# One core, attention and maxout feed-forward interleaved: the written order of commands, and the engines of copies, casts and masks, set anew

## The chip, the core and the metric

The kernel runs on one core of a Trainium2 chip. Five engines work side by side, each on its own queue in the order of the program: TensorE (PE, with its weight loads PEld), VectorE (DVE), ScalarE (ACT), GpSimd (POOL) and SyncE (SP). DMAs are issued from the queues of SP, ACT and POOL. The metric is the device time of one execution in microseconds; the median of six runs before the change is 200.44 us (199.77 to 200.55).

## What is computed

Attention with two kinds of heads, then a feed-forward layer whose hidden values are the largest of three products.

```python
scores = q @ k.T / sqrt(64)                      # 4 batches, 8 heads, 768 positions, 64 wide
keep = causal                                    # heads 0, 2, 6 ("retrieval")
keep = causal & ((key < 4) | (query - key < 64)) # the other heads
a = exp(where(keep, scores, -1e9) - max); a /= sum(a)
x = (a @ v), heads side by side                  # 3072 x 512
h = max(x @ w1, x @ w2, x @ w3)                  # 3072 x 768
out = h @ w_out                                  # 3072 x 512
```

Which heads are of which kind is read from the input `is_retrieval`, on the chip.

## The kernel before

**Tiles and steps.** A step `t` (0 to 15) is one batch `b`, one half of the positions (384 of 768, `half`) and one group of four heads; `t = 4 b + 2 half + group`. Within a step, `i` (0 or 1) is a pair of heads. The scores of a step are cut into units `u`: two units in the first half, four in the second. The feed-forward part `ffn(b, half)` works on 384 tokens: 18 products of a weight (768 columns in six blocks, three weights) with x, each four matmuls of 384 columns into one PSUM bank (line 437, 0.65 us), then three output blocks of six matmuls of 512 columns (line 473, 1.3 us). A product of the first weight is copied to `acc` by ScalarE or VectorE (line 454); the other two are joined to it by a maximum on VectorE (line 457), the last of which is `hT`. For batch 0 all products with w0 come first, then those with w1, then w2; for the others the three weights take turns.

**The order is written out by hand.** Nothing is scheduled: `PROGRAM` is a list of commands, and each command puts its instructions at the end of the queues of the engines that it uses, at the moment at which it stands in the list. Every queue so follows the order of the list. The commands:

- `read`, `flags`, `far`, `em hp`, `m hp`: from `is_retrieval` the flags of the heads, and on VectorE (line 388) two masks of 128x512 for heads 2hp and 2hp+1. `em` builds masks that TensorE adds to the scores (batch 0, first half), `m` masks that are multiplied in later. `far` also has two small POOL copies.
- `cast h hp e`: k and q of pair hp of batch 0 from fp32 to fp16 (line 211), by the engines in `e`, k first: `a` ScalarE, `d` VectorE, `p` POOL. `turnp h hp e`: six transposes on TensorE (line 230) and the copies to `KQ` (line 238), one of 768 columns for one letter, two of 384 for two. `h` is the half. `ld 1 hp`: loads of k and q of two pairs of the second half, issued by POOL.
- `load b g`, `turn b g i part`: for batches 1 to 3, k and q loaded as fp16 (two POOL DMAs, line 250), and a block transpose on VectorE (line 266); four per group.
- `load_v b half` (three SP DMAs), `load_vp` (three POOL DMAs), `v t i e`: v cast to fp16 (line 503, first letter) and multiplied by the flags into `vf` (line 505, second letter).
- `w n`: POOL's load of weight n (768 KB; 3 is w_out).
- `s t u [i] [b]`: score matmuls (line 552) into PSUM tile `st` (two buffers; with `b` into the four shared banks) and the exponential by ScalarE (line 563) into `pt`. For t = 0 and 1 the masks are added first by matmuls (line 536).
- `k t i u e`: mask multiplied into `pt`, on VectorE or POOL (line 585).
- `av t i [D]`: product with v (line 601), reciprocal (line 609) and scaling (line 611) on VectorE to `x`; with `D` a DMA transpose of x issued by SP (line 620), without it `x t i e` turns it on TensorE (line 633) and copies it (line 637). `x` of the last pair puts `ffn(b, half)` into the feed-forward queue.
- `f 1 e`: the next piece of the feed-forward queue (a product, an output block, or the empty half of an output block), its copy by engine `e`.
- `idle n`: n matmuls of zeros (line 321), work that nobody uses. `gate`: an SP DMA that waits for an exponential.

The four PSUM banks are shared by the feed-forward products, the transposes, the `av` results and the `b` scores. The loads of the first pairs stand ahead of `PROGRAM`, in `FIRST`: pair 0, the flags, pair 1, pairs 2 and 3, then v of the first half, on the queues of SP and ACT.

Of the kernel before, what the change touches and what calls it, by code (L numbers as in the profile page):

```python
# [713 lines left out]
```

## Time and profile before

| | |
|---|---|
| median of 6 runs | 200.44 us (199.77 to 200.55) |
| the profiled execution | 199.77 us, of which the span of the trace is 198.0 us |
| TensorE busy | 187.4 us (95%) |
| VectorE, ScalarE, POOL busy | 147.6, 114.6, 98.5 us (75%, 58%, 50%) |
| chain that ended last | PE 81%, DMA 6%, DVE 5%, POOL 2%, ACT 2%, issue 2%, SPq 1% |
| moved by DMA | 26.48 MB, 134 GB/s on average, 262 GB/s from 10 to 20 us |

Busy time is the union of the instructions' spans on an engine. The timeline and the chain give start and length in us; `x12` is the number of instructions merged into one row; square brackets hold the idle time ahead of an instruction and what ended it. In the chain, a piece stands with what it released next. All times are from the start of the span.

### The profile page before, as it was taken

The page shows a single profiled execution, that of the slowest core. Times are in us where ns is not written, and L with a number is a line of the kernel's source. Part 1 is how long each engine was busy: PE and PEld are TensorE (multiplying, and loading weights), DVE is VectorE, ACT ScalarE, POOL GpSimd, SP SyncE. Part 2 cuts the span into 40 slices and gives each one's busy share as a digit, 9 for nine tenths or more (in the row PEclk, how much of TensorE's full clock was granted, in tenths as well). Part 3 has the DMA queues.
Part 4 walks back from the last instruction along what each step waited for, and adds up shares of the span by engine and source line. Part 5 has one row for each costly group of instructions (what it writes and reads, how often), then busy time and mean ns, then how long its engine had stood idle before and what let it go on. Part 6 is the DMA issues. An engine that isn't in the chain of part 4 may idle for free.

```text
span 198.0 us, 5122 instructions
## 1 busy us (share of the span) xinstructions
PE 187.4 (95%) x2059; PEld 108.6 (55%) x2059; DVE 147.6 (75%) x306; ACT 114.6 (58%) x169; POOL 98.5 (50%) x132
## 2 busy tenths in 40 slices
PE   0998899999999999999999999999999999999992
PEld 0556555655555457664555457564565475745552
DVE  3787978798599968873897989897687537665740
ACT  3599885577857788277743976236457474102021
POOL 4685995968995704737942486910163127000000
PEclk9999999999999999999999999999999999999999
DMA  5999999989999264939991330214821330013004
GB/s 184 269 252 273 209 240 210 212 118 250 222 167 194 69 203 95 180 83 186 248 187 37 94 109 0 43 23 124 205 35 40 108 94 20 19 51 131 3 0 159
DMA packets 43245, 26.48 MB, mean 134 GB/s; under 512 B 33558, under 2 KB 38230, under 8 KB 43222
## 3 DMA queue, kind: packets, MB, share of 16 engines
q1 hardware_dynamic: 37206, 15.01, 31.7%
q0 software_dynamic: 4784, 10.23, 26.4%
q10 hardware_dynamic: 1232, 0.92, 1.5%
q8 instruction: 16, 0.26, 0.6%
q14 instruction: 7, 0.06, 0.1%
HBM read 25.17 MB, written 6.29 MB: 159 GB/s over the span
## 4 chain that ended last, share of the span: by engine, by line
PE 81%; DMA 6%; DVE 5%; POOL 2%; ACT 2%; issue 2%; SPq 1%; POOLq 0%
PE yy L437 43%; PE yy L473 14%; PE st L552 10%; PE oacc L601 10%; PE yst L437 3%; DMA qs<-in_q_dram 3%; DMA ks<-in_k_dram 2%; DVE mk L388 1%; DVE x L611 1%; DMA out_dram<-ot 1%; ACT pt L563 1%; PE yst L473 1%; DVE hT L457 1%; ACT ot L479 1%; POOL pt L585 1%
## 5 line engine op out<-in xcount | busy, mean ns | idle before, releaser
L563 ACT ACTIVATE pt<-st 128x1024 f16<-128x1024 f32 (+3 forms) x99 | 82.8, 895 | 37.1 <-PE st L552 28.7
L585 POOL TENSOR_TENSOR pt<-pt,mk 128x512 f16<-128x512 f16 (+1 forms) x51 | 53.8, 1077 | 34.8 <-ACT pt L563 34.2
L437 PE MATMUL yy<-xT,w1t 128*128 128x384 f16 x180 | 36.0, 326 | 0.0
L437 PE MATMUL yy<-xT,w0t 128*128 128x384 f16 x180 | 35.8, 326 | 0.0
L437 PE MATMUL yy<-xT,w2t 128*128 128x384 f16 x180 | 35.8, 326 | 0.0
L457 DVE TENSOR_TENSOR acc<-yy,acc 128x384 f16<-128x384 f32 x45 | 24.9, 554 | 11.2 <-PE yy L437 4.9
L473 PE MATMUL yy<-woutt,hT 128*128 128x512 f16 (+1 forms) x138 | 31.7, 375 | 0.0
L552 PE MATMUL st<-KQ 32*128 32x384 f16 (+5 forms) x560 | 28.6, 279 | 0.4
L457 DVE TENSOR_TENSOR hT<-yy,acc 128x384 f16<-128x384 f32 x45 | 24.6, 556 | 4.2 <-PE yy L437 1.7
L601 PEld LDWEIGHTS <-pt 128*128 128x128 f16 x672 | 24.2, 97 | 5.2 <-issue 1.5
L266 DVE STREAM_TRANSPOSE KQ<-kq 128x384 f32<-128x384 f32 x24 | 25.5, 1134 | 0.0
L454 ACT CAST acc<-yy 128x384 f16<-128x384 f32 x29 | 13.9, 486 | 20.0 <-PE yy L437 16.8
L601 PE MATMUL oacc<-va,pt 128*128 128x65 f16 x352 | 25.0, 193 | 0.4 <-POOL pt L585 0.4
L437 PEld LDWEIGHTS <-w0t 128*128 128x128 f16 x192 | 17.9, 98 | 13.1 <-issue 1.7
L437 PEld LDWEIGHTS <-w2t 128*128 128x128 f16 x192 | 17.8, 98 | 12.0 <-DVE x L611 0.3
L437 PEld LDWEIGHTS <-w1t 128*128 128x128 f16 x192 | 17.1, 97 | 11.4 <-issue 1.2
L552 PEld LDWEIGHTS <-KQ 32*128 32x128 f16 (+1 forms) x560 | 12.1, 93 | 18.5 <-issue 12.6
L473 PEld LDWEIGHTS <-hT 128*128 128x128 f16 x150 | 13.9, 98 | 14.9 <-issue 0.4
L601 PE MATMUL oacc<-vf,pt 128*128 128x65 f16 x320 | 21.5, 193 | 0.2 <-DVE vf L505 0.2
L505 POOL TENSOR_TENSOR vf<-va,far 128x384 f16<-128x384 f16 x13 | 10.9, 843 | 17.6 <-DVE va L503 8.6
L611 DVE TENSOR_TENSOR x<-oacc,rc 128x384 f16<-128x384 f32 x32 | 17.8, 557 | 1.1
L585 DVE TENSOR_TENSOR pt<-pt,mk 128x512 f16<-128x512 f16 (+1 forms) x35 | 18.2, 542 | 0.0
(75 smaller groups left out, 139.6 us busy)
## 6 DMA issues: line engine op xcount, KB each, us to landing
out_dram<-ot SPq DMA_DIRECT2D x23, 256.0 KB, 2.2
vs<-in_v_dram SPq DMA_DIRECT2D x21, 256.0 KB, 4.4
kq<-in_k_dram POOLq DMA_DIRECT2D x6, 384.0 KB, 6.1
kq<-in_q_dram POOLq DMA_DIRECT2D x6, 384.0 KB, 7.6
qs<-in_q_dram ACTq DMA_DIRECT2D x4, 192.0 KB, 3.9
ks<-in_k_dram SPq DMA_DIRECT2D x4, 192.0 KB, 3.7
ks<-in_k_dram POOLq DMA_DIRECT2D x2, 384.0 KB, 6.9
qs<-in_q_dram POOLq DMA_DIRECT2D x2, 384.0 KB, 7.3
```

The costliest lines, as they stand in the source:

```text
L266: nc.vector.transpose(out=dst.rearrange("c (p j) -> c j p", j=n)[:, j0:j1], in_=src.rearrange("c (j i) -> c j i", i=R),)
L388: nc.vector.tensor_scalar(out=mk[:, h], in0=kept, scalar1=least[:, h : h + 1], scalar2=-30000.0 if early else None, op0=ALU.is_le if early ...
L437: nc.tensor.matmul(yy[:, 0:HALF], w_t[wi][:, ks, ni * P : (ni + 1) * P], xT[b, half][ks].rearrange("p a t -> p (a t)"), start=(ks == 0), s ...
L454: copy_out[0](out=acc[ni], in_=yy[:, 0:HALF])
L457: nc.vector.tensor_tensor(out=dst, in0=yy[:, 0:HALF], in1=acc[ni], op=ALU.max)
L473: nc.tensor.matmul(yo[:, 0:n], hT[ns][:, tb * P : (tb + 1) * P], woutt[:, ns, c : c + n], start=(ns == 0), stop=(ns == NNB - 1),)
L505: vf_engine.tensor_tensor(out=vf[j][:, hs, k0:k1, 0:D], in0=vs[:, hs, 0:1] if half == 0 else va[j][:, hs, k0:k1, 0:D], in1=far[:, hs, k0:k ...
L552: nc.tensor.matmul(sts[g // m][:, g % m, c0 : c0 + n * P], KQ[rows, 0, ki * P : (ki + 1) * P], KQ[rows, 1, t0 : t0 + n * P], start=(c0 == ...
L563: nc.scalar.activation(out=pts[t, i][:, u, h0 : h0 + m, 0:w], in_=st[:, :, 0:w], func=AF.Exp, scale=sc,)
L585: engine.tensor_tensor(out=x, in0=x, in1=m, op=ALU.mult)
L601: nc.tensor.matmul(o[:, qi, hl, 0 : D + 1], pt[:, u, hl, c : c + P], vv[:, 2 * hp + hl, ki, 0 : D + 1], start=(idx == 0), stop=(idx == len ...
L611: nc.vector.tensor_tensor(out=x, in0=o[:, :, :, 0:D], in1=rc.unsqueeze(3).to_broadcast([P, HB, 2, D]), op=ALU.mult,)
```

## The change

`PROGRAM` is written anew. It holds the same commands for the same steps, 471 of them, with the same loads and the same tiles; what differs is their order and the engine letters of `cast`, `turnp`, `v`, `k`, `x` and `f`. No function changes. The new text is a line shorter, so lines of the code after it stand one lower (line 437 becomes 436).

Counted by letters, before to after: casts of k and q ScalarE 4 to 6, VectorE 5 to 4, POOL 7 to 6; casts of v ScalarE 5 to 12, VectorE 9 to 3, POOL 18 to 17; `vf` VectorE 10 to 8, POOL 22 to 24; `k` commands VectorE 31 to 26, POOL 43 to 48; `f` commands ScalarE 99 to 106, VectorE 93 to 86; `x` ScalarE 8 to 5, VectorE 4 to 7; copies to `KQ` of 384 columns ScalarE 10 to 2 and VectorE 2 to 6, of 768 columns ScalarE none to 3 and VectorE 2 to 1.

In order: the idle matmuls come ahead of the flags; `s 0 0 0` comes ahead of the first `s 1`; `ld 1 2` comes ahead of the first weight, `load_vp 0 1` ahead of `w 2`, `load 1 0` ahead of `w 3`; `turnp 1 2` and `turnp 1 3` come ahead of the first `f`; the `turn` commands of group (1, 0) come ahead of the first output block; `av 14 1` moves behind `av 15 0`.

```diff
 PROGRAM = (
-    "read, flags, cast 0 0 pa, cast 0 1 ad, cast 0 2 pp, em 0, turnp 0 0 aa, em 3, idle 8, far",
-    "ld 1 0, cast 0 3 ap, turnp 0 2 aa, em 2, turnp 0 1 dd, s 1 0 0, s 0 0 0, s 0 1 0 b, em 1",
-    "w 0, turnp 0 3 d, s 0 0 1, ld 1 2, s 1 1 0 b, s 0 1 1 b, v 0 1 dd, s 1 0 1, v 1 1 dd",
-    "s 1 1 1, v 0 0 dp, cast 1 1 pp, w 1, turnp 1 1 aa, cast 1 0 da, av 0 1, av 0 0, idle 2",
-    "av 1 1, turnp 1 0 aa, m 0, v 1 0 pp, s 2 0 1, w 2, av 1 0, s 2 0 0, x 1 1 d, x 1 0 d",
-    "x 0 1 d, x 0 0 a, s 2 1, m 1, m 2, m 3, cast 1 3 pd, f 1 d, load_vp 0 1, w 3, f 1 a, f 1 a",
-    "turnp 1 3 aa, cast 1 2 dd, load 1 0, f 1 d, s 2 2, k 2 1 1 p, f 1 a, k 2 0 1 p",
-    "turnp 1 2 d, f 1 d, k 2 0 2 d, f 1 a, s 3 0, k 3 0 0 d, f 1 d, f 1 d, s 2 3, k 2 1 2 p",
-    "f 1 d, f 1 a, f 1 d, k 2 0 3 d, load 1 1, f 1 a, v 2 1 pp, f 1 d, f 1 d, v 2 0 ad",
-    "v 3 1 ap, k 2 1 3 p, f 1 a, s 3 1 0, s 3 2 0, av 2 0 D, v 3 0 pp, s 3 1 1, f 1 d, av 2 1 D",
-    "k 3 0 1 p, f 1 a, turn 1 0 0 0, k 3 1 0 p, s 3 3 0, turn 1 0 0 1, turn 1 0 1 0, s 3 2 1",
-    "f 1 a, load_v 1 0, f 1 d, k 3 0 2 p, k 3 0 3 p, turn 1 0 1 1, f 1 a, k 3 1 1 p, s 3 3 1",
-    "k 3 1 2 p, gate, av 3 0, s 4 0, k 3 1 3 p, turn 1 1 0 0, f 1 a, av 3 1, turn 1 1 0 1",
-    "x 3 0 a, f 1 a, turn 1 1 1 1, k 4 0 0 p, x 3 1 a, f 1 d, k 4 1 0 p, s 4 1, f 1 a",
...
+    "cast 0 0 da, cast 0 3 pp, read, idle 8, flags, idle 2, em 3, ld 1 0, em 0, cast 0 1 aa",
+    "turnp 0 0 a, cast 0 2 aa, em 2, ld 1 2, s 0 0 0, far, turnp 0 1 a, em 1, w 0, v 0 0 pp",
+    "turnp 0 3 da, s 0 0 1, turnp 0 2 d, s 0 1 0 b, w 1, s 1 0 0, s 0 1 1 b, s 1 0 1, s 1 1 0 b",
+    "v 1 0 ad, cast 1 1 pp, cast 1 0 dd, v 0 1 ap, v 1 1 dp, turnp 1 0 dd, av 0 0, s 1 1 1",
+    "turnp 1 1 ad, av 1 0, cast 1 2 ap, load_vp 0 1, s 2 0 0, x 0 0 d, av 1 1, s 2 0 1, av 0 1",
+    "x 1 1 a, x 1 0 d, x 0 1 d, turnp 1 2 a, s 2 1, m 1, cast 1 3 pd, m 0, w 2, turnp 1 3 dd",
+    "k 2 0 1 p, m 3, f 1 d, s 3 0, f 1 a, k 2 1 1 p, f 1 a, s 2 2, load 1 0, f 1 d, m 2",
+    "k 3 0 0 d, f 1 a, k 2 1 2 d, f 1 d, f 1 d, s 2 3, k 2 0 2 p, w 3, f 1 a, s 3 1 0, f 1 d",
+    "f 1 a, k 2 1 3 p, v 2 0 ad, s 3 2 0, k 3 0 1 d, f 1 d, s 3 3 0, k 2 0 3 d, f 1 d, f 1 a",
+    "f 1 d, f 1 d, v 3 0 pp, v 2 1 pp, s 3 1 1, k 3 0 3 p, s 3 2 1, turn 1 0 0 1, load 1 1",
+    "f 1 d, turn 1 0 0 0, k 3 0 2 p, f 1 a, turn 1 0 1 0, turn 1 0 1 1, k 3 1 1 p, v 3 1 ap",
+    "f 1 a, av 2 0 D, av 3 0, s 3 3 1, av 2 1 D, s 4 0, gate, k 3 1 2 p, turn 1 1 0 0",
+    "k 3 1 3 p, k 3 1 0 p, load_v 1 0, load_v 2 0, f 1 a, av 3 1, s 4 1, turn 1 1 0 1, f 1 d",
+    "turn 1 1 1 0, x 3 0 a, f 1 a, turn 1 1 1 1, f 1 d, x 3 1 a, f 1 a, k 4 1 0 d, f 1 d",
...
+    "f 1 d, s 7 0, k 6 0 2 d, k 6 0 3 d, f 1 a, v 7 0 pp, load 2 1, f 1 a, f 1 a, v 7 1 ap",
+    "turn 2 0 1 0, s 7 1, k 6 1 1 p, turn 2 0 0 0, f 1 a, load_v 2 1, x 5 1 d, k 7 1 1 p, f 1 a",
+    "f 1 a, f 1 a, v 9 0 pd, v 8 0 dp, v 6 0 pp, k 6 1 2 p, turn 2 0 0 1, f 1 a, turn 2 0 1 1",
+    "s 7 2, f 1 a, f 1 a, load 3 1, f 1 d, k 7 1 2 p, f 1 d, turn 2 1 1 0, v 6 1 pp, s 7 3",
+    "f 1 a, load_v 3 0, av 6 0 D, f 1 d, k 7 1 3 p, f 1 a, f 1 a, f 1 d, k 7 0 2 p, f 1 a",
+    "f 1 a, s 8 0, turn 2 1 0 0, turn 2 1 0 1, f 1 a, k 7 0 1 p, k 7 0 3 p, f 1 d, turn 2 1 1 1",
+    "av 7 1 D, f 1 d, s 8 1, av 7 0 D, k 6 1 3 p, av 6 1 D, s 9 0, k 8 0 1 p, v 11 0 pd",
...
+    "f 1 d, k 15 1 3 p, f 1 a, f 1 a, f 1 d, f 1 d, k 15 0 1 p, k 15 0 2 p, f 1 d, av 15 1 D",
+    "f 1 d, av 15 0 D, av 14 1 D, x 15 1 a, f 1 a, f 1 a, f 1 d, f 1 a, f 1 a, f 1 d, f 1 a",
...
```

## The prediction

> **What bounds the kernel now.** I read the page first (busy shares and slices), then the busy time by stretches of 10 us, then the timeline and the chain of the first 50 us, then the landing times of the loads.
>
> ```profile
> span 198.0 us, 5122 instructions
> PE 187.4 (95%) x2059; PEld 108.6 (55%) x2059; DVE 147.6 (75%) x306; ACT 114.6 (58%) x169; POOL 98.5 (50%) x132
> ```
>
> The busy time by stretches (length, then PE, PEld, DVE, ACT, POOL, granted clock, DMA share, GB/s):
>
> ```profile
> 0.00:10.00 10.00, 5.26 (x36) 3.08 (x37) 5.54 (x23) 4.58 (x9) 5.35 (x17) 1.00 0.93 227
> 10.00:20.00 10.00, 9.23 (x128) 5.68 (x128) 7.75 (x22) 9.74 (x18) 6.71 (x12) 1.00 1.10 262
> 20.00:30.00 10.00, 9.12 (x79) 5.03 (x76) 8.77 (x20) 8.40 (x14) 9.58 (x12) 1.00 1.13 225
> 30.00:40.00 10.00, 9.84 (x117) 6.05 (x117) 7.73 (x16) 5.39 (x8) 7.38 (x9) 1.00 1.14 211
> 40.00:50.00 10.00, 9.53 (x122) 5.49 (x121) 9.43 (x14) 7.80 (x13) 7.75 (x9) 1.00 0.99 193
> 50.00:60.00 10.00, 10.00 (x124) 5.55 (x121) 7.37 (x16) 6.87 (x11) 9.92 (x16) 1.00 0.96 187
> ```
>
> From 50 us to 190 us TensorE is busy without a gap, and this work doesn't change. So only two things can move the end: how late the first 50 us leave TensorE, and a new gap after them. In the first 50 us ScalarE is full between 10 and 20 us (9.74 of 10) and the DMA engines are full throughout (share 0.93 to 1.14). The timeline (start, us, engine) and then the chain show the places that matter:
>
> ```profile
> 5.33 3.15 PE L321 MATMUL st<-zero 128*128 128x512 f16 x8
> 8.32 0.33 PE L230 MATMUL tr<-ident,kn 128*128 128x128 f16 x3
> 10.03 5.94 ACT L563 ACTIVATE pt<-st 128x1024 f16<-128x1024 f32 x11 [0.48 <-PE st L552]
> 20.71 2.11 PE L437 MATMUL yy<-xT,w0t 128*128 128x384 f16 x12
> 31.86 0.50 POOL L503 CAST va<-vs 128x384 f16<-128x384 f32 x1 [2.27 <-DMA vs<-in_v_dram]
> 45.36 0.20 PE L601 MATMUL oacc<-va,pt 128*128 128x65 f16 x1 [0.38 <-POOL pt L585]
> ```
> ```profile
> 34.94 0.83 DVE vf L505
> 44.15 1.17 POOL pt L585
> 48.34 2.17 PE yy L437 x12
> ```
>
> The reader is to see: the first exponential starts at 10.03; the products of the feed-forward part start at 20.71; the second v load is late (POOL waits 2.27 us for it at 31.86), so that `av 2 0` waits on VectorE's `vf`; and `av 3 1` waits on a POOL mask at 45. The row at 48.34 is the first product of `ffn(0,1)`; its first matmul stands at 48.28. In both programs the same TensorE work lies ahead of that product, so its start is my yardstick.
>
> The landing of a load is its issue (timeline) plus its time to landing (view of the tile):
>
> ```profile
> L402 POOL DMA_DIRECT2D w2t<-in_moe_w_dram x1: 803/803/803, 16.8 to 16.8; - x1
> DMA to landing us min/median/max: 11.6/11.6/11.6
> ```
>
> So w2 landed at 28.4; likewise w0 18.7, w1 24.6, the POOL v loads 29.6 to 31.7, woutt 35.2, the last early kq 42.8. These loads queue behind each other: 1.1 us per 256 KB, 3.3 to 4.1 per weight of 768 KB, 1.9 per kq.
>
> **The change part by part.** An engine that has work waiting starts its next instruction before the last one ends, so I take start-to-start times from back-to-back rows: ScalarE exponential of 1024 columns 0.92 (row 1.02), of 256 0.26, cast or copy of 384 columns 0.37 to 0.42; VectorE cast 0.46, max 0.47, block transpose 0.92 (row 1.13), reciprocal with multiply 0.70; POOL mask of 512 1.11, of 256 0.62, cast 0.46 to 0.53, `vf` 0.79, DMA issue 0.8 (0.55 for kq).
>
> *Start.* The eight idle matmuls (and the two that took 0.59 us at 16.2) move ahead of the first transposes, into time in which TensorE waited 4.6 us for its first work: they cost nothing there. Pair 0 is cast by VectorE and ScalarE at 4.0 to 4.9, turned at 5.6 (behind two more idle matmuls), copied by ScalarE at 6.4 to 7.15 behind two casts of pair 1, and `s 0 0 0` no longer waits for pair 2. Its exponential follows the casts of pair 2 at 7.9, 2.1 us earlier than 10.03. The row: eight idle matmuls took 3.15 us (about 0.42 apart), and 3.6 us after the first work at 4.7 the transposes ran at 0.056 apart. The Trainium skill (TensorE: Matmul & The Clock Gate, Part 1) says some 3.4 us of sustained work opens the full clock, with a window that runs freely. By the page's rule the first transposes of after may still be slow; six of them at 0.107 instead of 0.056 would be 0.3 us, which the wait for pair 1 on ScalarE covers.
>
> ScalarE pays for it. Ahead of the exponentials of `s 2 1` it casts six k or q tiles (four before: 0.84 more) and two v tiles (none before: 0.84); its copies are eight of 384 columns before (2.96), and three of 768 and two of 384 after. No row has a ScalarE copy of 768: the exponential of 768 (0.71) and two copies of 384 (0.74) bound it from above, one of 384 (0.37) from below; I take 0.7, the nearest in size, so 2.8 in all. I walked the queues in their new order with the times above. ScalarE: casts 5.95, copy 6.4, casts 7.06 and 7.48, exponential 7.9, copies 8.8 and 9.5, exponential 10.25, two short ones 11.2, then 12.1 (VectorE's copy of pair 2 ends at 11.55), 13.0, 13.55, 14.5 to 15.0, v casts to 15.8, then a wait to 17.0 because TensorE stands before `turnp 1 0` for qn, whose load is issued 0.7 us later than before (behind the casts of pair 3 on POOL, 9.0 instead of 8.3) and lands near 15.1; `s 2 0` at 18.3 and 19.2; `s 2 1` at 21.75. The first product starts at 22.3 (20.71 before, but with 0.68 us less TensorE work ahead of it): at this point after is 0.9 us behind.
>
> *Loads.* `ld 1 2` now stands ahead of w0, and the v loads ahead of w2 and woutt. POOL issues them at 10.6, w0 at 12.4, w1 at 14.0, v at 17.9, w2 at 21.0, kq at 25.0, woutt at 28.4. At the queue's rate: w0 21.0 to 21.4 (used 22.3), w1 24.7, v 25.8 to 28 (used 31), w2 31.6 to 32.3 (used 33.4), kq 35.3, woutt 38.8 (used 41.7). None is late, w0 and w2 by about 1 us only; the 2.27 us wait for v is gone.
>
> *22 to 48 us.* Walking TensorE with 0.66 per product, 0.54 per whole score group, 0.27 per single pair, 0.95 per `av`, 1.3 per output block: it waits 0.7 us before `s 3 0` (VectorE copies pair 3 only after two mask builds), reaches product (1,3) with its end at 31.5, `s 3 1 1` at 35.4, `av 2 0` at 38.0. VectorE has four block transposes between the last maxima, so the last hT is ready at 41.0; TensorE fills that time with three `av`. `s 4 0` ends at 41.7, the output blocks and `av 3 1` follow (POOL's last mask for it, after 11.2 us of POOL work from 30.4, ends at 41.6; needed at 43.0), and `ffn(0,1)` starts at 47.3. Before: 48.28. Gain 1.0 us. What it gains against product (1,3), where it's 0.35 behind, is the two waits shown above (`vf`, POOL mask) and the smaller ones around them.
>
> *After 48 us.* Masks, casts and copies change engines all over (POOL 48 masks for 43, VectorE 26 for 31; ScalarE 106 `f` for 99). TensorE's work is the same, and a later producer costs only if it comes after TensorE wants it. The tightest place: v 7 1 is a ScalarE cast placed after the second output block of `ffn(0,1)`, near 67.0 (47.3 and 19.7 of TensorE work). From its `vf` on (0.8) POOL has nine masks (10.0), two whole v preparations (2.5), two half ones (0.8) and a kq issue (1.15) in a row, 15.3 us, up to the end of mask `k 6 1 3`, which `av 6 1` wants right away, after 16.4 us of TensorE work, near 83.5. The mask ends at 82.7. Cost nothing, cover 0.8 us; if that cover is gone, what is over comes straight onto TensorE. The bound by rows: masks at 1.09 (the fastest) save 0.2, at 1.18 (the mean row) add 0.6. SBUF — State Buffer of the Trainium skill (section on ports) speaks against the change here: POOL shares a port pair with VectorE, held for a whole instruction. If the masks met this more often and ran at 1.25, 1.3 us would come on top and 0.5 would be lost; by the rows nothing is lost.
>
> At the end `av 14 1` is now the last one whose transpose goes by DMA; 4.55 us of TensorE work cover it against 0.75 on VectorE, a short queue on SP and 2.3 to 2.7 to landing. Cost nothing, cover about 0.9. The last 24 steps are the same.
>
> **Sum.** The profiled execution took 199.77 us (span 198.0 and 1.77 around it). Less 1.0 gives 198.8. The median of six runs, 200.44, is 0.67 above it, so I forecast 199.5 for the median: 1.0 earlier with 0.1 given back in the narrow places. 0.2% (0.4 us) is about what a measurement of this kernel can tell from no change.
>
> **The rivals.**
>
> *ScalarE and VectorE pay their full rows (slower).* Place: 8 to 45 us. If each instruction occupies its engine for its row (exponential 1.02, transpose 1.13, cast 0.51) the same walk has the last hT at 43.9 and `ffn(0,1)` at 49.7, 1.4 us later than before: 201.8. For it: 1.7 us more ScalarE work, and four block transposes more (two reciprocals with multiplies fewer) on VectorE ahead of the last hT. Against: eleven exponentials took 5.94 us at 10.03, less than their rows' 7.1. Between 1.0 earlier and 1.4 later it decides from about 40% of the difference between row and spacing.
>
> *POOL late near 83 us, or w2 late (no change).* A chain 10% longer or w2 a microsecond later takes 0.7 to 1.0 off: 200.2 to 200.5.
>
> *The start counts in full.* If `turnp 1 0` isn't held by its load, the 0.9 us behind at the first product fall away: about 198.4.
>
> *It doesn't matter.* If TensorE's filler hides start and v wait alike, 200.4. Against: TensorE has no spare after 50 us, so what it loses before stays lost.
>
> **How the numbers follow.** Forecast (198.8 to 200.0) 0.46; full start 0.10; no change by POOL, w2 or otherwise 0.17; slower by the row-length case or an unseen gap 0.27. The range takes in 198.4 and the slower rival short of its end: 198.3 to 201.7. Faster by over 0.2% 0.57, within it 0.16, slower 0.27.
>
> **What would show it.** First exponential near 7.9 instead of 10.0; first product near 22.3; no wait for v on POOL; `ffn(0,1)` near 47.3; TensorE busy 10.00 in every stretch from 50 to 180. Wrong if w0 or w2 is awaited by TensorE, if `yy` waits on VectorE around 37 to 42, or if `av 6 1` waits on POOL near 83.

## The result, and the profile after

The change made no difference that can be measured, where 199.5 us and a gain were forecast. The ratio of the times, after to before, is 1.0016 (95% interval 1.0000 to 1.0032). The median of before over 72 runs is 200.31 us. Of the 36 runs of after, the profiled one among them, 13 were disturbed (202.6 to 206.3 us, 11 of them at a mean granted clock of 0.98 to 0.992); the median of the 23 others is 200.29 us, and the times of the kernels below leave such runs out. The profiled execution of after took 200.29 us with a span of 198.6; before's took 199.77 and 198.0. So against the execution on which the forecast was summed, after is 0.5 us later instead of 1.0 us earlier.

The head of the page of after:

```profile
span 198.6 us, 5124 instructions
PE 189.1 (95%) x2059; PEld 108.4 (55%) x2059; DVE 147.4 (74%) x296; ACT 117.2 (59%) x173; POOL 102.1 (51%) x136
```

The busy time of after by stretches (columns as before), and behind it two stretches of before:

```profile
0.00:10.00 10.00, 7.08 (x41) 3.10 (x41) 5.21 (x23) 6.00 (x11) 3.31 (x12) 1.00 0.91 226
10.00:20.00 10.00, 8.39 (x116) 4.87 (x113) 7.04 (x15) 8.97 (x18) 8.84 (x17) 1.00 0.98 231
20.00:30.00 10.00, 9.06 (x79) 4.86 (x80) 8.44 (x19) 8.64 (x13) 7.95 (x10) 1.00 1.12 223
30.00:40.00 10.00, 10.00 (x101) 5.63 (x99) 9.93 (x19) 6.64 (x9) 8.59 (x11) 1.00 1.16 209
40.00:50.00 10.00, 10.00 (x153) 6.25 (x153) 9.85 (x20) 6.95 (x12) 4.51 (x5) 1.00 0.68 138
...
60.00:70.00 10.00, 10.00 (x128) 5.20 (x126) 9.85 (x20) 7.50 (x11) 3.34 (x6) 1.00 0.96 167
70.00:80.00 10.00, 9.58 (x100) 5.38 (x98) 5.20 (x10) 7.13 (x11) 9.83 (x14) 1.00 1.02 215
```
```profile
60.00:70.00 10.00, 10.00 (x104) 4.89 (x102) 9.93 (x20) 7.89 (x10) 5.94 (x7) 1.00 0.60 129
70.00:80.00 10.00, 10.00 (x140) 6.44 (x140) 7.61 (x17) 7.69 (x11) 2.91 (x4) 1.00 0.59 139
```

Two things are to be seen. From 30 to 50 us TensorE has no gap left (10.00 and 10.00, where before had 9.84 and 9.53): the waits there are gone, as forecast. And there is a new gap between 70 and 80 us, 9.58, where before was full. The DMA share at 60 to 70 us is 0.96; in before it was 0.60.

The yardstick, the first matmul of `ffn(0,1)`, and the products around it in the timeline of after:

```profile
22.95 0.81 PE L436 MATMUL yy<-xT,w0t 128*128 128x384 f16 x4
48.26 1.46 PE L436 MATMUL yy<-xT,w0t 128*128 128x384 f16 x8
78.55 0.81 PE L436 MATMUL yy<-xT,w0t 128*128 128x384 f16 x4
79.78 0.82 PE L436 MATMUL yy<-xT,w1t 128*128 128x384 f16 x4 [0.42 <-DVE x L610]
```

First product 22.95 (forecast 22.3, before 20.71 with 0.68 us less work ahead of it), `ffn(0,1)` 48.26 (forecast 47.3, before 48.28). The gap at 79.78 is ended by VectorE's `x` of `av 6 0`, which frees a PSUM bank. The chain of after, followed through that gap:

```profile
57.56 9.54 DMA vs<-in_v_dram
...
67.84 0.82 POOL vf L504
68.66 0.55 POOL kq L249
69.21 8.74 DMA kq<-in_q_dram
...
78.90 0.25 DVE rc L608
79.17 0.57 DVE x L610
...
79.78 2.12 PE yy L436 x12
```

and VectorE's block transpose in the timeline:

```profile
77.98 1.13 DVE L265 STREAM_TRANSPOSE KQ<-kq 128x384 f32<-128x384 f32 x1 [1.82 <-DMA kq<-in_q_dram]
```

So: a v load lands at 67.1; POOL, which had waited for it, prepares that v and only then issues the loads of kq (2,1); they land at 77.95; VectorE's block transpose waits 1.82 us for them, with `rc` and `x` of `av 6 0` queued behind it; TensorE waits for the bank.

To split the time I use the yardstick and the first matmul of the last output block of the kernel. The TensorE work between them is the same in every kernel here, and so is the work ahead of the first. The two ends in before, and then the second in after:

```profile
48.28 2.24 PE L437 MATMUL yy<-xT,w0t 128*128 128x384 f16 x12
193.00 0.82 PE L473 MATMUL yst<-woutt,hT 128*128 128x256 f16 x6
```
```profile
193.55 0.82 PE L472 MATMUL yst<-woutt,hT 128*128 128x256 f16 x6
```

Before needs 193.00 - 48.28 = 144.72 us from one to the other, after 193.55 - 48.26 = 145.29 us.

### The profile page after: what moved, and what is told of

Read it like the earlier page. It is cut to its first block, busy times and chain, and to the rows that moved or that the text cites. A ratio compares the mean times of both kernels' runs of the same rounds, so it can differ in the third digit from the quotient of the medians.

```text
span 198.6 us, 5124 instructions
## 1 busy us (share of the span) xinstructions
PE 189.1 (95%) x2059; PEld 108.4 (55%) x2059; DVE 147.4 (74%) x296; ACT 117.2 (59%) x173; POOL 102.1 (51%) x136
## 4 chain that ended last, share of the span: by engine, by line
PE 73%; DMA 14%; DVE 3%; ACT 2%; SPq 2%; issue 2%; POOL 2%; POOLq 0%; DVEq 0%; ACTq 0%
PE yy L436 38%; PE yy L472 13%; PE oacc L600 9%; PE st L551 8%; DMA vs<-in_v_dram 5%; DMA kq<-in_q_dram 4%; PE yst L436 3%; DMA ks<-in_k_dram 3%; DMA qs<-in_q_dram 2%; ACT pt L562 1%; DVE x L610 1%; PE yst L472 1%; SPq L285 1%; DVE KQ L237 1%; DVE va L502 1%
## 5 line engine op out<-in xcount | busy, mean ns | idle before, releaser
L584 POOL TENSOR_TENSOR pt<-pt,mk 128x512 f16<-128x512 f16 (+1 forms) x55 | 58.8, 1089 | 41.1 <-ACT pt L562 36.0
L456 DVE TENSOR_TENSOR acc<-yy,acc 128x384 f16<-128x384 f32 x45 | 24.4, 554 | 13.2 <-ACT acc L453 6.3
L472 PE MATMUL yy<-woutt,hT 128*128 128x512 f16 (+1 forms) x138 | 32.2, 375 | 0.0
L265 DVE STREAM_TRANSPOSE KQ<-kq 128x384 f32<-128x384 f32 x24 | 26.0, 1127 | 1.8 <-DMA kq<-in_q_dram 1.8
L600 PE MATMUL oacc<-vf,pt 128*128 128x65 f16 x320 | 20.9, 193 | 0.0
L584 DVE TENSOR_TENSOR pt<-pt,mk 128x512 f16<-128x512 f16 (+1 forms) x31 | 16.2, 547 | 0.9 <-ACT pt L562 0.6
L502 POOL CAST va<-vs 128x384 f16<-128x384 f32 x17 | 9.2, 544 | 11.5 <-DMA vs<-in_v_dram 11.5
```

The source lines that it names most:

```text
L265: nc.vector.transpose(out=dst.rearrange("c (p j) -> c j p", j=n)[:, j0:j1], in_=src.rearrange("c (j i) -> c j i", i=R),)
L456: nc.vector.tensor_tensor(out=dst, in0=yy[:, 0:HALF], in1=acc[ni], op=ALU.max)
L472: nc.tensor.matmul(yo[:, 0:n], hT[ns][:, tb * P : (tb + 1) * P], woutt[:, ns, c : c + n], start=(ns == 0), stop=(ns == NNB - 1),)
L502: op(out=vdst, in_=vs[:, hs])
L584: engine.tensor_tensor(out=x, in0=x, in1=m, op=ALU.mult)
L600: nc.tensor.matmul(o[:, qi, hl, 0 : D + 1], pt[:, u, hl, c : c + P], vv[:, 2 * hp + hl, ki, 0 : D + 1], start=(idx == 0), stop=(idx == len ...
```

## The experiments

**1. Which half of the list loses (c1, c2).** c1 has after's commands up to `x 3 1` and then before's; c2 has before's up to `x 3 1` and then after's. The seams (in kernels put together from two lists, line numbers stand one or two off those of after):

```diff
 c1, against after
-    "k 3 1 3 p, k 3 1 0 p, load_v 1 0, load_v 2 0, f 1 a, av 3 1, s 4 1, turn 1 1 0 1, f 1 d",
-    "turn 1 1 1 0, x 3 0 a, f 1 a, turn 1 1 1 1, f 1 d, x 3 1 a, f 1 a, k 4 1 0 d, f 1 d",
+    "gate, k 3 1 2 p, turn 1 1 0 0, k 3 1 3 p, k 3 1 0 p, load_v 1 0, f 1 a, av 3 1, s 4 1",
+    "turn 1 1 0 1, f 1 d, turn 1 1 1 0, x 3 0 a, f 1 a, turn 1 1 1 1, f 1 d, x 3 1 a, f 1 a",
+    "k 4 0 0 p, f 1 d, k 4 1 0 p, f 1 a, load_v 1 1, f 1 a, v 4 0 pp, k 4 0 1 d, k 4 1 1 p",
...
 c2, against before
-    "x 3 0 a, f 1 a, turn 1 1 1 1, k 4 0 0 p, x 3 1 a, f 1 d, k 4 1 0 p, s 4 1, f 1 a",
-    "turn 1 1 1 0, load_v 1 1, f 1 a, v 4 0 pp, k 4 0 1 d, k 4 1 1 p, f 1 a, s 5 0, v 4 1 pp",
+    "f 1 a, av 3 1, turn 1 1 0 1, x 3 0 a, f 1 a, turn 1 1 1 1, k 4 0 0 p, x 3 1 a",
+    "load_v 2 0, s 4 1, turn 1 1 1 0, k 4 1 0 d, f 1 d, f 1 a, k 4 1 1 d, f 1 a, s 5 0, f 1 a",
...
```

Expected of c1:

> The commands of after up to `x 3 1` (without `load_v 2 0`, which keeps its place of before), then those of before that are left. Theory A (the new start and middle gain nothing by 48 us, and all of the loss, 0.6 us, comes from one wait near 79 us that belongs to after's later order): `ffn(0,1)` begins near 48.3 as in before (48.28), no gap of TensorE near 79, span 197.9 to 198.2, ratio to before 0.999 to 1.001. Rival B (the loss is made by the start, where ScalarE and VectorE got more work, and only shows later): span 198.4 to 198.7, ratio 1.002 to 1.004. Rival C (the start gains the 1.0 us that was forecast, and the later order loses more): span near 197.0, ratio near 0.995.

Expected of c2:

> The commands of before up to `x 3 1`, then those of after that are left. Theory A: `ffn(0,1)` near 48.3, then the same gap of about 0.55 us near 79 as in after, where VectorE's block transpose waits for the kq load: span 198.4 to 198.7, ratio 1.002 to 1.004. Rival B: span near 198.0, no gap, ratio 0.999 to 1.001. Rival C: span near 199.5, ratio near 1.008.

Measured: c1 199.06 us, ratio 0.9948 (0.9923 to 0.9972), span 196.9, `ffn(0,1)` at 46.93. c2 201.23 us, ratio 1.0056 (1.0024 to 1.0088), span 199.7, `ffn(0,1)` at 49.02. My theory A, drawn from the one trace of after, fell with c1 (c2's interval alone leaves both A and C open); rival C stood: the head gains the forecast 1.0 us, and the later order loses about as much. Multiplied, the two ratios make 1.0004, within the interval of after's. In c2 the stretch from the yardstick to the last block takes 145.66 us, 0.94 more than before. It has two waits of TensorE, neither of them at the place of after's: one for a copy by ScalarE just behind the seam, and one for a DMA transpose of x.

```profile
50.95 0.64 PE L553 MATMUL st<-KQ 32*128 32x384 f16 x16 [0.34 <-ACT acc L455]
...
72.58 0.48 PE L438 MATMUL yy<-xT,w0t 128*128 128x384 f16 x2 [0.32 <-DMA xT<-x]
```

**2. Take away the late kq (c3, c7).** c3 issues kq (2,1) ahead of the POOL command that waits for v; c7 leaves POOL alone and exchanges two v loads on SP, so that the v POOL waits for comes first.

```diff
 c3, against after
-    "f 1 d, s 7 0, k 6 0 2 d, k 6 0 3 d, f 1 a, v 7 0 pp, load 2 1, f 1 a, f 1 a, v 7 1 ap",
+    "f 1 d, s 7 0, k 6 0 2 d, k 6 0 3 d, f 1 a, load 2 1, v 7 0 pp, f 1 a, f 1 a, v 7 1 ap",
...
 c7, against after
-    "k 3 1 3 p, k 3 1 0 p, load_v 1 0, load_v 2 0, f 1 a, av 3 1, s 4 1, turn 1 1 0 1, f 1 d",
+    "k 3 1 3 p, k 3 1 0 p, load_v 1 0, load_v 1 1, f 1 a, av 3 1, s 4 1, turn 1 1 0 1, f 1 d",
...
-    "k 5 1 0 d, f 1 a, s 5 1, f 1 d, f 1 a, v 4 0 pp, load_v 1 1, v 4 1 pp, av 4 0 D, s 6 0",
+    "k 5 1 0 d, f 1 a, s 5 1, f 1 d, f 1 a, v 4 0 pp, load_v 2 0, v 4 1 pp, av 4 0 D, s 6 0",
```

> After with `load 2 1` ahead of `v 7 0` instead of behind it; nothing else. Theory A (POOL's wait of 6.5 us for v holds the issue of the kq load, whose late landing at 78.0 stops VectorE's block transposes, with `rc` and `x` of `av 6 0` behind them): the two kq DMAs are issued near 61 instead of 68.6, land by 71, the block transposes don't wait, the gap of TensorE near 79 is gone; span 0.5 to 0.6 less than after's 198.6, so 198.0 to 198.1, ratio to before 0.999 to 1.001. Rival D (VectorE is late there by its own work, four block transposes and the mask builds, not by the load): gap stays at 0.3 or more, span 198.4 to 198.6.

> After with `load_v 1 1` and `load_v 2 0` exchanged, so that SP issues v of (1,1) first; the POOL commands keep their order, `load 2 1` behind `v 7 0`. Theory A, one step further back (v of (1,1) is late because v of (2,0), used 20 us later, stands ahead of it on SP): v of (1,1) lands before 57, POOL's 6.5 us wait at `v 7 0` is gone, kq is issued near 62, the gap near 79 is gone: span 198.0 to 198.1, ratio 0.999 to 1.001. Rival E (the loads' rate holds it, whatever the order): wait of 3 us or more stays on POOL, span 198.3 or more. Rival D as above: wait gone, gap stays.

Measured: c3 200.44 us, ratio 1.0015 (0.9989 to 1.0041); c7 200.74 us, ratio 1.0014 (0.9983 to 1.0045). The gap near 79 us went in both, as theory A said, and nothing was won: another one opened nine microseconds earlier. The timeline of c3:

```profile
70.64 0.69 PE L436 MATMUL yy<-xT,w0t 128*128 128x384 f16 x2 [0.81 <-DMA xT<-x]
71.74 0.48 PE L436 MATMUL yy<-xT,w0t 128*128 128x384 f16 x2 [0.41 <-DMA xT<-x]
```

The first product of `ffn(1,0)` now waits 1.2 us for the DMA transposes of x (in c7 0.53 and 0.42 us at the same place). From the yardstick to the last block c3 takes 146.47 and c7 146.15 us, longer than after's 145.29. Rivals D and E named no such thing either. What c3 and c7 have in common with after is the traffic; which transfer ends last changes with the order. In after, POOL's stall had kept the kq load out of the way of the transposes: they land 2.3 to 3.5 us after their issue there, 3.7 to 4.7 us in c3 and 5.2 to 7.1 us in c7.

The queue that issues both shows where the traffic comes from. SP's commands of before, and then of after, from the timeline (start and length of the issuing, and at the end of a row the number of DMAs in it):

```profile
48.95 2.91 SPq L286 DMA_DIRECT2D vs<-in_v_dram  x3
56.47 11.36 SPq L620 DMA_TRANSPOSE xT<-x  x4
```
```profile
46.39 6.78 SPq L285 DMA_DIRECT2D vs<-in_v_dram  x6
53.26 2.14 SPq L479 DMA_DIRECT2D out_dram<-ot  x3
55.59 7.20 SPq L285 DMA_DIRECT2D vs<-in_v_dram  x3
62.88 5.95 SPq L619 DMA_TRANSPOSE xT<-x  x4
```

After issues nine v DMAs of 256 KB between 46 and 63 us; before issues six, the last of them by 51.9. The three more are `load_v 2 0`, which before issues at 71.25, behind the transposes. In after they stand ahead of `load_v 1 1`, whose v is wanted first. The three of `load_v 1 1` take 7.20 us to issue, 2.91 in before, and the transposes come behind them on the same queue. (DMA: Bandwidth & Descriptors of the Trainium skill, under "Issuing engines are not separate DMA queues", says that DMAs from the scalar, sync and gpsimd queues run on the same 16 engines and interleave. c3 agrees: with a load moved earlier on POOL's queue, TensorE waits 1.2 us for transposes that were issued on SP's queue.)

**3. Take that load out of the stretch (c8, c11).** Both move `load_v 2 0` behind the transposes of step 5. Its first users must move with it: in c8 to behind `k 6 1 3`, in c11 only to ahead of `load 3 1`.

```diff
 c8 and c11, against after
-    "k 3 1 3 p, k 3 1 0 p, load_v 1 0, load_v 2 0, f 1 a, av 3 1, s 4 1, turn 1 1 0 1, f 1 d",
+    "k 3 1 3 p, k 3 1 0 p, load_v 1 0, f 1 a, av 3 1, s 4 1, turn 1 1 0 1, f 1 d",
...
-    "f 1 a, f 1 a, s 6 2, av 4 1 D, k 6 0 1 p, f 1 a, av 5 1 D, f 1 d, s 6 3, av 5 0 D, f 1 a",
+    "f 1 a, f 1 a, s 6 2, av 4 1 D, k 6 0 1 p, f 1 a, av 5 1 D, f 1 d, s 6 3, av 5 0 D, load_v 2 0, f 1 a",
...
-    "f 1 a, f 1 a, v 9 0 pd, v 8 0 dp, v 6 0 pp, k 6 1 2 p, turn 2 0 0 1, f 1 a, turn 2 0 1 1",
+    "f 1 a, f 1 a, v 6 0 pp, k 6 1 2 p, turn 2 0 0 1, f 1 a, turn 2 0 1 1",
 c8
-    "av 7 1 D, f 1 d, s 8 1, av 7 0 D, k 6 1 3 p, av 6 1 D, s 9 0, k 8 0 1 p, v 11 0 pd",
+    "av 7 1 D, f 1 d, s 8 1, av 7 0 D, k 6 1 3 p, v 9 0 pd, v 8 0 dp, av 6 1 D, s 9 0, k 8 0 1 p, v 11 0 pd",
 c11
-    "s 7 2, f 1 a, f 1 a, load 3 1, f 1 d, k 7 1 2 p, f 1 d, turn 2 1 1 0, v 6 1 pp, s 7 3",
+    "s 7 2, f 1 a, f 1 a, v 9 0 pd, v 8 0 dp, load 3 1, f 1 d, k 7 1 2 p, f 1 d, turn 2 1 1 0, v 6 1 pp, s 7 3",
```

> After with `load_v 2 0` taken from its place behind `load_v 1 0` (48 us) to behind `av 5 0`'s transpose (near 67 us), and its first users on POOL and VectorE, `v 9 0` and `v 8 0`, from 73 us to behind `k 6 1 3`. Theory F (the three loads of v of (2,0), 768 KB in the stretch from 48 to 70 us that before does not have there, cost after 0.5 to 1.2 us in whichever transfer ends last: kq of group (2,1) when it is issued late, the DMA transposes of steps 4 and 5 when kq is issued early): v of (1,1) lands before 58, POOL's wait at `v 7 0` under 1 us, transposes land by 69 and kq by 70, no gap of TensorE over 0.3 between 60 and 85; from the start of `ffn(0,1)` to the end the kernel takes 0.5 us less than after (4.4 us more than the bare TensorE work there, so 3.8 to 4.0); span 197.0 to 198.3 by how the start falls, ratio to before 0.993 to 0.998. Rival G (the later order loses by its engines' work, the masks, casts and block transposes that were moved, not by loads): a gap of 0.4 or more stays or comes elsewhere, ratio 1.000 to 1.004.

> After with `load_v 2 0` from behind `load_v 1 0` (48 us) to behind `av 5 0`'s transpose (near 66 us), and `v 9 0 pd, v 8 0 dp` only some commands later, to ahead of `load 3 1` (near 74 us, when that v has landed); no engine letter changes and VectorE's stretch from 80 to 98 us is left as in after. Theory F (loads): neither the gap near 79 nor a wait for the DMA transposes near 70; from the start of `ffn(0,1)` to the end 3.8 to 4.1 us over the bare TensorE work (after 4.42, c3 5.59, c7 5.28, before 3.84); ratio to before 0.994 to 0.998. Rival G (the new places of masks, casts and block transposes on VectorE and POOL cost it): gaps of 0.4 us or more in sum between 60 and 100 with no load or DMA transpose in their chain, ratio 1.000 to 1.005.

Measured: c8 201.60 us, ratio 1.0052 (1.0027 to 1.0077). There is no gap of TensorE between 60 and 85 us, as theory F said, but the ratio is far from its 0.993 to 0.998. My placing had made two new ones:

```profile
90.08 0.39 PE L472 MATMUL yy<-woutt,hT 128*128 128x512 f16 x1 [0.97 <-DVE hT L456]
...
96.52 0.36 PE L600 MATMUL oacc<-va,pt 128*128 128x65 f16 x6 [0.67 <-DVE x L610]
```

I had put a cast and a `vf` on VectorE at 86 us, into a stretch where it works from 80 to 98 us almost without a pause. That run alone could not tell F from rival G. c11, where VectorE's part comes at 74 us, could: 199.42 us, ratio 0.9950 (0.9918 to 0.9981), span 197.2, and from the yardstick to the last block 144.69 us, as in before. Its stretches and POOL's rows at the place of the old stall:

```profile
60.00:70.00 10.00, 10.00 (x124) 5.25 (x117) 8.70 (x18) 7.94 (x11) 3.38 (x6) 1.00 0.90 156
70.00:80.00 10.00, 10.00 (x105) 5.92 (x103) 7.83 (x14) 6.30 (x10) 9.83 (x13) 1.00 1.13 224
```
```profile
60.19 0.50 POOL L502 CAST va<-vs 128x384 f16<-128x384 f32 x1 [0.24 <-DMA vs<-in_v_dram]
60.77 0.83 POOL L504 TENSOR_TENSOR vf<-va,far 128x384 f16<-128x384 f16 x1
61.54 0.59 POOL L249 DMA_DIRECT2D kq<-in_k_dram  x1
```

POOL waits 0.24 us for v instead of 6.48, issues kq at 61.5 instead of 68.6, and neither kq nor the transposes are awaited. One load placed later, with two commands that use it, turns after into a kernel 0.5% faster than before. That load is the cause of after's loss behind the yardstick. The two commands moved with it do not make the wait: in after VectorE's part of them runs at 68.5 us, and VectorE idles for 1.82 us ahead of its late block transpose; POOL's part runs at 72.8, behind the issue of that kq. The moved masks, casts and copies (G) cost nothing that is seen after 48 us in c11. By the traces the load costs 0.6 us (145.29 - 144.69); the ratios of after and c11, which were measured at different times, lie 1.3 us apart. How much of the rest is a later start of after's runs (48.26 against 47.43 at the yardstick in the two traces) is not shown.

**4. The same load early in another order (c16).** c4 (next experiment) is before with its first v loads earlier; c16 is c4 with `load_v 2 0` behind `load_v 1 1`.

```diff
 c16, against c4
-    "turn 1 1 1 0, load_v 1 1, f 1 a, v 4 0 pp, k 4 0 1 d, k 4 1 1 p, f 1 a, s 5 0, v 4 1 pp",
+    "turn 1 1 1 0, load_v 1 1, load_v 2 0, f 1 a, v 4 0 pp, k 4 0 1 d, k 4 1 1 p, f 1 a, s 5 0, v 4 1 pp",
...
-    "f 1 a, s 7 2, load_v 2 0, f 1 d, f 1 a, f 1 a, av 6 0 D, v 7 1 ap, s 7 3, load 3 1",
+    "f 1 a, s 7 2, f 1 d, f 1 a, f 1 a, av 6 0 D, v 7 1 ap, s 7 3, load 3 1",
```

> The kernel c4 (before with the early v loads; 199.52, TensorE almost without gaps) with `load_v 2 0` moved from 71 us to behind `load_v 1 1` (51 us), nothing else: the 768 KB alone, in a kernel whose engines' order is that of before. Theory F: kq of the groups (2,0) and (2,1) and the DMA transposes of steps 4 and 5 land 2 to 3.3 us later (kq near 66 instead of 63.7, transposes near 68 to 70 instead of 67), VectorE's first block transpose of batch 2 or the products of `ffn(1,0)` at 70.3 wait: 0.3 to 1.5 us lost, ratio to before 0.997 to 1.003. Rival L (these places have room enough in before's order; it needs after's order too): within 0.2 us of c4, ratio 0.994 to 0.996.

Measured: 199.77 us, ratio 0.9946 (0.9913 to 0.9978). The trace has the wait of theory F, with a small price: 145.12 us from the yardstick to the last block, where c4 takes 144.71, and of these 0.41 us

```profile
71.16 0.32 PE L437 MATMUL yy<-xT,w0t 128*128 128x384 f16 x1 [0.30 <-DMA xT<-x]
```

The ratio does not differ from c4's 0.9947. It lies in L's range and outside F's, which the interval only just reaches; the 0.41 us of the trace is at the low end of F's 0.3 to 1.5. Behind `load_v 1 1` the extra load costs at most a few tenths; the 0.6 to 1.7 us of after, c3 and c7 need after's order as well.

**5. The price of the v wait in the head (c4, c12).** c4 is before with only `load_vp 0 1` ahead of `w 2`; c12 takes c1 and puts it back behind `w 2`.

```diff
 c4, against before
-    "av 1 1, turnp 1 0 aa, m 0, v 1 0 pp, s 2 0 1, w 2, av 1 0, s 2 0 0, x 1 1 d, x 1 0 d",
-    "x 0 1 d, x 0 0 a, s 2 1, m 1, m 2, m 3, cast 1 3 pd, f 1 d, load_vp 0 1, w 3, f 1 a, f 1 a",
+    "av 1 1, turnp 1 0 aa, m 0, v 1 0 pp, s 2 0 1, load_vp 0 1, w 2, av 1 0, s 2 0 0, x 1 1 d, x 1 0 d",
+    "x 0 1 d, x 0 0 a, s 2 1, m 1, m 2, m 3, cast 1 3 pd, f 1 d, w 3, f 1 a, f 1 a",
...
 c12, against c1
-    "s 1 1 1, turnp 1 1 ad, av 1 0, cast 1 2 ap, load_vp 0 1, s 2 0 0, x 0 0 d, av 1 1",
+    "s 1 1 1, turnp 1 1 ad, av 1 0, cast 1 2 ap, s 2 0 0, x 0 0 d, av 1 1",
...
-    "w 2, turnp 1 3 dd, k 2 0 1 p, m 3, f 1 d, s 3 0, f 1 a, k 2 1 1 p, f 1 a, s 2 2",
+    "w 2, load_vp 0 1, turnp 1 3 dd, k 2 0 1 p, m 3, f 1 d, s 3 0, f 1 a, k 2 1 1 p, f 1 a, s 2 2",
```

> Before with `load_vp 0 1` moved ahead of `w 2`, nothing else: the price of the v wait alone. By the prediction's walk the wait of 2.27 us on POOL costs TensorE only the 0.16 us at `av 2 0` and part of the 0.38 us for the last mask: gain 0.2 to 0.5 us, ratio 0.9975 to 0.999, if w2 landing 2.8 us later (near 31) stays in time for its first product at 32.2. Rival: w2 is late, its first product waits, ratio 1.002 or more.

> The kernel c1 (head of after, rest of before; 199.06) with `load_vp 0 1` put back behind `w 2`, where before has it: v lands near 31.5 instead of 28 and is wanted near 30.6 (ScalarE) and 31.0 (POOL). If the early v loads are what the head of after gains: 0.3 to 1.0 us lost, ratio to before 0.997 to 1.000. Rival: the head gains by its other edits (`turnp 1 2` and `turnp 1 3` ahead of the first products, masks and block transposes placed earlier) and the wait is hidden: within 0.2 us of c1, ratio 0.994 to 0.996.

Measured: c4 199.52 us, ratio 0.9947 (0.9921 to 0.9974); w2 is not late. By its ratio, which is better than the expected 0.9975 to 0.999, this one move gains as much as the whole head of after. The trace shows only part of that: `ffn(0,1)` at 47.97 instead of 48.28, 0.31 us, inside the expectation. The runs of before spread from 199.36 to 201.93 us beside it, those of c4 from 199.34 to 199.94, and before's profiled execution, 199.77, is the fastest of the first six. Why the ratio says more than the trace stays open. The second trace with before's head, c2, reaches `ffn(0,1)` only at 49.02, but POOL waits 1.93 us for that v there, no longer than in before; its extra lateness is there by 24.8 us, ahead of the use of that v. c12: 200.39 us, ratio 0.9995 (0.9967 to 1.0023), against c1's 0.9948. In its trace ScalarE waits for that v:

```profile
33.02 0.51 ACT L504 CAST va<-vs 128x384 f16<-128x384 f32 x1 [1.04 <-DMA vs<-in_v_dram]
```

and it needs 25.82 us from the first product (22.91) to `ffn(0,1)` (48.73), where c1 needs 25.25. So the early v loads are the larger part of the head's gain, 0.57 us by the trace (25.82 - 25.25) and 0.9 by the ratios.

**6. VectorE's mask builds ahead of the first product (c9).** c8 with `m 1` and `m 0` behind `turnp 1 3`.

```diff
 c9, against c8
-    "x 1 1 a, x 1 0 d, x 0 1 d, turnp 1 2 a, s 2 1, m 1, cast 1 3 pd, m 0, w 2, turnp 1 3 dd",
+    "x 1 1 a, x 1 0 d, x 0 1 d, turnp 1 2 a, s 2 1, cast 1 3 pd, w 2, turnp 1 3 dd, m 0, m 1",
```

> The kernel of the run before this one with the builds of masks `m 1` and `m 0` moved behind `turnp 1 3` on VectorE. Theory H (those four builds stand ahead of the cast and the copy that `turnp 1 3` needs, the wait of 0.4 to 0.5 us for `qn` just ahead of the first product): that wait is gone and the first product 0.3 to 0.5 us earlier against the exponentials of `s 2 0`; ratio 0.002 below the run before this one. Rival I (the wait is for the cast's load or for ScalarE's copy of `turnp 1 2`): no difference.

Measured: 201.54 us, ratio 1.0059 (1.0027 to 1.0090), against c8's 201.60 and 1.0052. The wait of TensorE just ahead of the first product (0.33 us in c8) is gone, as H said, and a longer one stands right behind that product:

```profile
22.13 0.81 PE L436 MATMUL yy<-xT,w0t 128*128 128x384 f16 x4
...
23.96 0.40 PE L551 MATMUL st<-KQ 64*128 64x384 f16 x4 [0.52 <-ACT pt L562]
```

From the first product to `ffn(0,1)` it needs 26.03 us, c8 25.38. The masks held nothing that ScalarE's exponentials did not hold as well.

c9 shows one thing more. `load_v 2 0` stands late in it, as in c8 and c11, and still TensorE waits for a DMA transpose of x:

```profile
71.38 0.48 PE L436 MATMUL yy<-xT,w0t 128*128 128x384 f16 x2 [0.46 <-DMA xT<-x]
```

From the yardstick to the last block c9 takes 147.30 us, c8 146.68. So after's order has little cover at this place even with the load late; c8 and c11 show no wait there.

**7. Is after's start slower by its engine work? (c10, c14, c18).** All three start with before's commands up to about `s 2 1` and go on with after's. The remaining kernel is c8 for c10, after's middle and before's end for c14, c11 for c18.

```diff
 c10
     "em 1, w 0, turnp 0 3 d, s 0 0 1, ld 1 2, s 1 1 0 b, s 0 1 1 b, v 0 1 dd, s 1 0 1",
...
     "x 1 1 d, x 1 0 d, x 0 1 d, x 0 0 a, s 2 1, cast 1 2 ap, turnp 1 2 a, m 1, cast 1 3 pd",
 c14, against c10
-    "em 1, w 0, turnp 0 3 d, s 0 0 1, ld 1 2, s 1 1 0 b, s 0 1 1 b, v 0 1 dd, s 1 0 1",
+    "em 1, ld 1 2, w 0, turnp 0 3 d, s 0 0 1, s 1 1 0 b, s 0 1 1 b, v 0 1 dd, s 1 0 1",
 c18, against c14
-    "idle 2, av 1 1, turnp 1 0 aa, m 0, v 1 0 pp, s 2 0 1, load_vp 0 1, w 2, av 1 0, s 2 0 0",
-    "x 1 1 d, x 1 0 d, x 0 1 d, x 0 0 a, s 2 1, cast 1 2 ap, turnp 1 2 a, m 1, cast 1 3 pd",
+    "idle 2, av 1 1, turnp 1 0 aa, m 0, v 1 0 pp, s 2 0 1, cast 1 2 ap, load_vp 0 1, w 2",
+    "av 1 0, s 2 0 0, x 1 1 d, x 1 0 d, x 0 1 d, x 0 0 a, turnp 1 2 a, s 2 1, m 1",
```

> The commands of before up to `s 2 1` (with the v loads `load_vp 0 1` ahead of `w 2`), then those of the first kernel of this call that are left. By the walk of the prediction the start of after is 0.9 us behind at the first product for its ScalarE work; theory J (true): first product 0.5 or more earlier than with after's start in the same call, near 21.9 with 9.6 us of bare TensorE work ahead of it, `ffn(0,1)` near 47.2, span 196.6 to 197.2, ratio 0.991 to 0.996. Rival K (the start is set by how the first loads land, the order of casts does not matter): first product between 22 and 23, ratio within 0.001 of the first run's.

> The commands of before up to `s 2 1` with the v loads ahead of `w 2` and `ld 1 2` ahead of `w 0` (the miss of the run c10 mended: there `cast 1 2` waited 2.26 us for that load), then after's up to `x 3 1` (without `load_v 2 0`), then before's. If after's start is behind for its ScalarE and VectorE work (prediction: 0.9 us at the first product, 0.35 at the product (1,3)): 0.3 to 0.6 us faster than c1, median 198.5 to 198.8, ratio 0.991 to 0.994, and less spread from run to run than c1's 1.9 us. Rival: the start of after costs nothing against before's, ratio within 0.001 of c1's 0.995.

> The commands of before up to `x 0 0`, with `ld 1 2` ahead of `w 0`, the v loads ahead of `w 2` and `cast 1 2` ahead of `s 2 0` (in c10 and c14 it stood behind the exponentials of `s 2 1` on ScalarE, which cost 2.26 us); from there the commands of c11 (after with the late `load_v 2 0`). If after's start is behind for its ScalarE and VectorE work: first product of the w0 block (1) at 12.3 to 12.9 us over the bare TensorE work, where kernels with after's start have 12.83 to 14.38 (mean 13.6); ratio to before 0.990 to 0.993. Rival (the start of after costs nothing against before's, what differs is how the first loads land): 13.0 to 14.0 there, ratio 0.994 to 0.997.

Measured: c10 204.26 us (1.0169, 1.0118 to 1.0219), c14 202.21 us (1.0058, 1.0014 to 1.0103). Both tell nothing of the question, because of the same wait, here in c10:

```profile
23.89 0.34 PE L231 MATMUL tr<-ident,kn 128*128 128x128 f16 x3 [2.26 <-ACT kn L212]
```

I first read this as a late load and mended that in c14; the wait stayed, 2.27 us there. (Behind it the granted clock was 0.50, from 25 to 27 us in c10 and from 24 to 30 us in c14.) The cast `kn` stood behind the two exponentials of `s 2 1` on ScalarE, where my splice had put it. With the cast ahead of them, c18 took 199.75 us, ratio 0.9966 (0.9945 to 0.9986). Its first product with w1 starts at 28.57 with 14.37 us of bare TensorE work ahead of it (by my count of the instructions at their back-to-back spacing), so 14.20 us of waiting: the rival's side, even above its 14.0. The six traces with after's head (table below) have the same product at 27.19 to 28.75. With after's middle, before's start gains nothing; a part of that is a wait of 1.07 us for VectorE's `x` that this mix has of its own. The question is answered only so far.

## Why the prediction was wrong

**The sum failed in one step: "After 48 us".** There I walked masks, casts and the one POOL chain, named a place near 83 us and wrote "Cost nothing, cover 0.8 us". The loads I walked only up to woutt. `load_v 2 0` stands in the diff beside `load_v 1 0`, some 20 us ahead of its time in before (71.25), and `load 2 1` behind `v 7 0` on POOL; neither was costed, and SP's queue was not walked past 48 us. The terms put at nothing were the traffic of that load and the waits behind it, POOL's for v and SP's queue for the transposes; the sum gave back 0.1 us for all narrow places. Before's own rows would have given the warning: a DMA share of 0.96 from 50 to 60 us, and my own 1.1 us per 256 KB, so 3.3 us for 768 KB. The runs put the price at 0.57 us in after's trace (145.29 - 144.72), 1.43 in c7, 1.75 in c3, part of the 0.94 in c2, and at nothing without that load there in c11; c9 shows how narrow that is. With c11's ratio the forecast time would have come out: 0.9950 of 200.3 is 199.3.

**The head was right, on the mean of the traces.** Six kernels have after's head unchanged as far as the yardstick's work goes:

| | first product | `ffn(0,1)` | between them |
|---|---|---|---|
| c1 | 21.68 | 46.93 | 25.25 |
| c8 | 21.75 | 47.13 | 25.38 |
| c3 | 22.04 | 47.40 | 25.36 |
| c11 | 22.18 | 47.43 | 25.25 |
| after | 22.95 | 48.26 | 25.31 |
| c7 | 23.22 | 48.49 | 25.27 |

The means are 22.30 and 47.61, forecast 22.3 and 47.3. With before's head unchanged there are two traces, 48.28 and 49.02. So a gain of 1.0 us at the yardstick (48.65 - 47.61) is what the head brings, on few traces that differ by 0.7 to 1.6 us among themselves, and c1 shows it at the end. One of the six has a cause of its own: in c7 the granted clock is 0.50 from 10 to 13 us (1.00 in the five others); without it the means are 22.12 and 47.43. After's own trace is one of the late ones: 0.65 us late against my walk at the first product. From there on it needs 25.31 us for which I had 25.0.

So the profiled execution comes out as the forecast's 198.8, plus 0.65 (start of this execution), plus 0.3 (middle), plus 0.55 (new waits after 48 us): 200.3, measured 200.29. That explains this one execution, and its late start is bad luck. After's median is the same 200.29; where the other runs lost their time, no trace shows.

Point by point:

- First exponential 7.9: 8.35 in after, 7.91 in c1. It waits for casts behind the first k and q loads, whose landing differs from run to run. Right, with a spread I had not given.
- TensorE held before `turnp 1 0`: yes, 0.81 us in after, 0.65 to 0.81 in c1, c3, c8 and c11. POOL issued that load at 9.34 instead of 9.0, because its cast of pair 3 began only at 8.44.
- The 0.9 us behind at the first product: 2.24 later than before in after, less 0.68 of work, is 1.56; on the mean of the six 0.9. That it is ScalarE's work was only argued; in after's trace the largest waits at 17 to 23 us are for VectorE (0.50 and 0.40 us), and c18 does not support it.
- The loads up to woutt: none awaited by TensorE, though each landed 1 to 2 us after my time (w0 12.80 + 9.5 = 22.3, w2 21.74 + 11.4 = 33.1).
- "The 2.27 us wait for v is gone": that one yes. But the view of waits of after has 11.5 us of POOL waiting for v, in two pieces that end at 52 and 67 us. I had forecast none. The first (5.07 us) held nobody whom TensorE waited for; the second led to the gap.
- POOL's chain near 83: the masks ended at 85.33 instead of 82.7, since the chain began late, and `av 6 1` was not held. The named place was harmless.
- The rule weighed there, SBUF — State Buffer of the Trainium skill on the port pair of POOL and VectorE: no sign of it. POOL's masks of 512 columns took 1167 ns on the mean, 1183 in before, not 1250.
- The clock rule (TensorE: Matmul & The Clock Gate of the Trainium skill, Part 1): the first transposes ran 0.057 apart at 5.48, 4.2 us after the first idle matmul at 1.26. That agrees with the page, and my 0.3 us of slow transposes did not come.
- The tail (`av 14 1`): no wait in any trace.
- Rivals: the time came out in the range of "no change", but not by its mechanism, neither a POOL chain at 83 us nor w2. What came is the "unseen gap" to which a part of the 0.27 for "slower" was given. That 200.29 lies in the stated range is the width of that range and no merit of the walk. The row-length rival (`ffn(0,1)` at 49.7) was wrong: 46.9 to 48.5.

## What to carry to other kernels

When an order is rewritten, walk the loads to the end of the kernel and not only the engines, and write beside each load the time of its first use: a load 20 us early need not be free (0.4 us in c16, 0.6 to 1.7 us in after's order): it takes DMA time from the transfers that are wanted first and stands ahead of them on its queue. When the removal of a wait wins nothing, look just ahead of it in the next trace: here the two waits (kq, DMA transposes) took turns, and only less traffic in that stretch removed both. Before the sum is set against one execution, see how much the start alone moves from run to run: here 1.5 us at the first product, which in after's head went through to the yardstick undiminished.

## What the runs showed that was not expected

The six traces of the same head start their first product between 21.68 and 23.22 us, and then take between 25.25 and 25.38 us to the yardstick: all the spread arises in the first 23 us, and no wait up to the yardstick absorbs any of it. In c7 it is partly the clock (0.50 from 10 to 13 us); the other five spread over 1.27 us. This holds for after's head, not for every head: c4 and c16 have the same commands up to the yardstick, start their first product at 21.41 and 20.27, and both reach the yardstick at 47.97 and 47.95. There waits behind the first product took up all of 1.14 us.

DMAs issued from SP can hold its queue much longer in one stretch than in another: three v DMAs of 256 KB took 2.91 us to issue in before, 7.20 in after and 8.03 in c3. Transposes of x behind them waited for their queue as well as for their transfer.

The best versions of this study are c1 (199.06 us, 0.9948), c11 (199.42 us, 0.9950), c4 (199.52 us, 0.9947) and c16 (199.77 us, 0.9946). They cannot be told apart, and all four are 0.5% faster than before.
